# A planner for attention beside a gated FFN: later exponentials, limited chains, a load in seven parts

## The chip, the core and the metric

The kernel runs on one core of a Trainium2 chip. The core has five engines, each with its own instruction stream: TensorE (PE in the profile, with PEld for its weight loads) multiplies matrices into PSUM, VectorE (DVE) and ScalarE (ACT) read PSUM and SBUF, GpSimd (POOL) and SyncE (SP) here mostly issue DMAs. The engines run side by side and meet at semaphores. Within one stream the order is fixed when the program is built: an instruction that waits holds up all that stand behind it.

The metric is device time in microseconds. Thirteen runs of the kernel before gave a median of 865.38 us, from 860.25 to 869.33.

## What is computed

```python
qkv = (x @ wqkv).reshape(B, S, 3, H, Dh)          # S 2048, D 512, H 32, Dh 16
p = softmax(q @ k.T * Dh ** -0.5)                  # 32 heads of 2048 x 2048
a = (p @ v).reshape(B, S, D) @ wo
b = (silu(x @ w_gate) * (x @ w_up)) @ w_down       # F 1792
g = sigmoid((x * gate_w).sum(-1, keepdims=True))
out = g * a + (1 - g) * b
```

The heads are narrow (16), so the 32 x 2048 x 2048 exponentials outweigh the matmuls: 134 million elements of softmax on a core whose engines handle 128 of them side by side.

## The kernel before, in words

**Units, slots, blocks.** The queries are cut into 4 blocks of 512, the heads into 8 groups of 4. A unit is one query block with one head group; there are 32 (`UNIT`, L114). A unit has 16 slots, one for each 128 keys, so `SLOTS` is 512. A slot has four score blocks of 128 keys x 512 queries, one for each head. `score` (L656) is one matmul of 64 rows; two heads sit in the two row halves of the array, so two such matmuls run side by side.

**Two ways to an exponential.** `emit_pair` (L669) puts two score blocks into one PSUM tile `s_t` (two buffers) and lets ACT take the exponential of 128 x 1024 elements at once into `e_t` (ten buffers). `emit_d` (L688) puts a block into one of the three spare PSUM banks as `d_t`, and DVE makes the exponentials of a whole slot (128 x 2048) itself: four steps y_t<-d_t, one for each block, which scale the scores into the bits of a bf16; then the correction z_t, u_t<-z_t, two 128 x 2048 products, a DMA of POOL that adds u_t onto y_t, and a last step y_t<-y_t. The scratch u_t changes place from one tile to the next: a buffer of its own, or by turns another tensor that is not in use yet or any more: `wd_t[:, 0:4]` up to unit 4, then `kaug[:, 0]` (L712).

**What each unit ends with.** `pv` (L774) multiplies the exponentials of a slot with V (o_ps<-e_t or o_ps<-y_t, four heads side by side). After 16 slots `close` (L1047) copies o_ps into osb on DVE, and SP copies the rows of osb to where they are needed.

**Chains.** All other matmuls are cut into pieces of one or two matmul steps and put between the score pairs: projections of K, V and Q for later units (`k_pieces`, L393; its copy goes to `kst`, for most groups the tensor `on`, and eight DMAs on SP bring it into `kaug`, L420), the bounds of the exponents, the gate, the FFN's gate and up products (`gu_chain`, L596, 8 steps in two banks, then a tanh on ACT and two DVE steps gs and mt), the down products (`down_pieces`, L627, 28 steps in two banks) and the output projection (`fin_pieces`). `Pacer` gives every slot a credit, from the work that is left and its deadlines. A chain with a tanh needs ACT between exponentials.

**The planner.** One Python loop (L1186 on) writes out the whole order for PE, ACT and DVE before anything runs; `ordered` (L145) then ties each instruction to the one before it on its engine. The loop keeps an estimate of when each engine is done (`plan.pe`, `plan.act`, `plan.dve`) from fixed durations: an exponential 0.905 us (`emit_pair`), a tanh 0.48 (`done_gu`, L608), DVE's steps 0.6 to 1.2. From these it decides how much fits between two score pairs (`room`, then `side`, L1108), when a bank is free (`m_tile`, `m_free`), when `pv` may go (`e_end`), and how many slots of a unit DVE takes: `v_unit` (L1153) gives DVE a slot only while DVE's estimated end, with 16 us to spare, lies before ACT's. So a changed duration changes the share of the work and the order on every engine.

The DMAs of SP and POOL are not tied this way. They stand in an order that follows from the program and from what they wait for, and each waits in its own queue for its operands and for one of eight completion semaphores, which go round. `wd_load` (L202, called from `begin`, L1089, at slot 88) fetches the down weights; it is later than it need be for the FFN because `wd_t[:, 0:4]` serves as scratch until then.

The lines that the change touches: `wd_load` L202, `done_gu` L608, `emit_pair` L669, the costs in `emit_d` L716 to L731, `begin` L1083, `side` L1108, `next_pv` L1130, and the main loop.

Of the kernel before, what the change touches and what calls it, by code (L numbers as in the profile page):

```python
# [8 lines left out]
ACT = mybir.ActivationFunctionType  # L9
# [69 lines left out]
def kernel(  # L79
# [12 lines left out]
    nc = tc.nc  # L92
# [66 lines left out]
    def act(*args, **kw):  # L159
        ordered(nc.scalar.activation(*args, **kw))  # L160
# [38 lines left out]
                h = H - 8 + 4 * i + j  # L199
                nc.sync.dma_start(out=wo_l[32 * j + 1:32 * j + 1 + DH, i, :], in_=A_wo[h * DH:(h + 1) * DH, :])  # L200

    def wd_load():  # L202
        nc.sync.dma_start(out=wd_t[:], in_=B_w_down.rearrange("(fc p) d -> p fc d", p=P))


    kaug = big.tile([P, G, S], BF16, name="kaug")
# [389 lines left out]
    def gu_chain(qb, fc):  # L596
        st = {}

        def load():
            st["wg"] = ffnw.tile([P, DC, P], BF16, tag="wg", name="wg")  # L600
            nc.sync.dma_start(out=st["wg"][:], in_=B_w_gate[:, fc * P:(fc + 1) * P].rearrange("(dc p) f -> p dc f", p=P))
            st["wu"] = ffnw.tile([P, DC, P], BF16, tag="wu", name="wu")
            nc.sync.dma_start(out=st["wu"][:], in_=B_w_up[:, fc * P:(fc + 1) * P].rearrange("(dc p) f -> p dc f", p=P))

        def rows(which):
            return lambda dc: (st["w" + which][:, dc, :], xT[:, dc, qb * QBW:(qb + 1) * QBW])

        def done_gu(gp, up):  # L608
            th = work.tile([P, QBW], BF16, tag="th", name="th")
            act(out=th[:], in_=gp[:, :], func=ACT.Tanh, scale=0.5)  # L610
            plan.act = max(plan.act, plan.pe + 0.25) + 0.48

            def gate():
                st["gs"] = work.tile([P, QBW], BF16, tag="gs", name="gs")
                vec.scalar_tensor_tensor(out=st["gs"][:], in0=th[:], scalar=1.0, in1=gp[:, :],
                                         op0=ALU.add, op1=ALU.mult)
                m_free(gp, plan.dve)

            def gated():
                vec.scalar_tensor_tensor(out=mt[:, fc, :], in0=st["gs"][:], scalar=0.5, in1=up[:, :],  # L620
                                         op0=ALU.mult, op1=ALU.mult)
                m_free(up, plan.dve)
            later(0.6, gate, plan.act + 0.2)
            later(0.6, gated, plan.act + 0.2)
        return load, two_banks(DC, "gu", rows("g"), rows("u"), done_gu)
# [43 lines left out]
    def emit_pair(bs):  # L669
        i = pairs[0] % 2  # L670
        s_t = ps_s.tile([P, 2 * QBW], F32, tag="s", name="s_t")
        e_t = etp.tile([P, 2 * QBW], BF16, tag="e", name="e_t")
        for k, b in enumerate(bs):
            score(s_t[:, k * QBW:(k + 1) * QBW], b)
            e_of[b] = e_t[:, k * QBW:(k + 1) * QBW]
        spend("R", 1, s_end[i])
        act(out=e_t[:], in_=s_t[:], func=ACT.Exp, scale=inv_sqrt_dh)
        plan.act = max(plan.act, plan.pe + 0.27) + 0.905
        s_end[i] = plan.act + 0.18
        for b in bs:  # L680
            e_end[b] = plan.act + 0.25
            e_left[b] = pairs[0]
        pairs[0] += 1

    d_wait = []
    y_live = [0]

    def emit_d():  # L688
        if not vcur:
            vcur.update(n=v_take(), i=0, y=vex.tile([P, NV * QBW], U16, tag="y", name="y_t", bufs=NY))  # L690
            y_live[0] += 1
        n, i, y = vcur["n"], vcur["i"], vcur["y"]
        vcur["i"] += 1
        d_t = m_tile("d_t")
        score(d_t[:, :], 4 * n + i)
        spend("R", 1)
        e_of[4 * n + i] = y[:, i * QBW:(i + 1) * QBW].bitcast(BF16)
        if i == NV - 1:
            vcur.clear()

        def first():
            vec.tensor_scalar(out=y[:, i * QBW:(i + 1) * QBW], in0=d_t[:, :], scalar1=EXP_A, scalar2=EXP_B,
                              op0=ALU.mult, op1=ALU.add)
            m_free(d_t, plan.dve)
            if i < NV - 1:
                return
            z = vex.tile([P, NV * QBW], U16, tag="z", name="z_t")
            u_turn[0] ^= 1
            if u_turn[0]:

                ua = (kaug[:, 0, :] if au > QB else wd_t[:, 0:4, :].rearrange("p f d -> p (f d)")).bitcast(F16)
            else:  # L712
                ua = vex.tile([P, NV * QBW], F16, tag="u", name="u_t")[:, :]
            ya, za = y[:, :], z[:, :]
            vops.extend([
                (0.66, lambda: vec.tensor_scalar(out=za, in0=ya, scalar1=0x1FF, scalar2=0x800, op0=ALU.bitwise_and,  # L716
                                                 op1=ALU.bitwise_or)),
                (0.66, lambda: vec.tensor_scalar(out=ua, in0=za, scalar1=EXP_K, scalar2=EXP_M, op0=ALU.mult,
                                                 op1=ALU.add)),
                (1.2, lambda: vec.tensor_tensor(out=ua, in0=ua, in1=ua, op=ALU.mult)),  # L720
            ])

            def add():
                vec.tensor_tensor(out=ua, in0=ua, in1=za, op=ALU.mult)
                nc.gpsimd.dma_start(out=ya, in_=ua, accum_op=ALU.add)  # L725
                added.append((plan.dve + ADD_US, last))

            def last():
                vec.tensor_scalar(out=ya, in0=ya, scalar1=EXP_D, scalar2=0.25, op0=ALU.add, op1=ALU.mult)
                vready.append((plan.dve + 0.4, n))  # L730
            vops.append((1.2, add))  # L731
        d_wait.append((plan.pe + 0.25, first))

    def pay_d():
# [348 lines left out]
    def begin(n):  # L1083
        plan.slot = n
        for c in need.get(n, []):
            force(c)
        if n == 28:
            late_loads()
        if n == (QB + 1) * KT + 8:  # L1089
            wd_load()  # L1090
        for f in at.pop(n, []):
            f()
        pace.begin_slot(n)
# [14 lines left out]
    def side(most):  # L1108

        due = any(not c.out() for n in range(plan.slot, plan.slot + 12) for c in need.get(n, []))  # L1110
        cur = pace.cur
        begun = cur is not None and not cur.out() and cur.i
        c = pick() if pace.credit > 0 or due or begun else None
        if c is None:
            return None
        mms, _, takes = c.pieces[c.i][:3]
        mode, two = c.pieces[c.i][3:] or ("F", None)
        if two and two["seq"] == plan.seq:
            return None
        t = m_ready(int(takes)) if takes else 0.0  # L1120
        if t is None or t > plan.pe + 0.1 or 0.226 * mms + (0.1 if plan.mode != mode else 0.0) > most:
            return None
        return c
# [4 lines left out]
        pace.credit -= emit_piece(c)  # L1128

    def next_pv():  # L1130
        while not pv_list(None):
            if vops:
                pay_v()
            elif d_wait:
                pay_d()
            elif owed:
                pay()
            elif added:
                pay_a()
            else:  # L1140
                emit_d()
        emit_pv(pv_list(None)[0])
# [43 lines left out]
    while au < UNITS:  # L1186
        if plan.slot < au * KT + at_ * KT // hi[au]:
            begin(plan.slot + 1)
            continue
        fill_dve()  # L1190
        back = pairs[0] - min(e_left.values(), default=pairs[0])
        if back >= EB - 1:
            next_pv()
            continue
        room = s_end[pairs[0] % 2] - plan.pe
        if room > 0.02:
            if want_d():
                emit_d()
                continue
            n_pv = pv_list(plan.pe)  # L1200
            switch = 0.0 if plan.mode == "C" else 0.1
            fits = int((room + SLACK - switch) / 0.216)
            c = side(room + SLACK)
            if n_pv and fits > 0 and (plan.mode == "C" or len(n_pv) > 1 and fits > 1 and (pv_turn[0] or c is None)
                                      or back >= EB - 4 or c is None and fits == 1):
                emit_pv(n_pv[0])
                pv_turn[0] = False
                continue
            if c is not None:
                put_piece(c)  # L1210
                pv_turn[0] = True
                continue
            if room > 0.15:
                plan.pe += 0.1
                continue
        n = au * KT + at_
        emit_pair([4 * n + 2 * half, 4 * n + 2 * half + 1])
        half ^= 1
        at_ += not half
        forward()  # L1220
    while closed < UNITS or vops or added or vcur:
        fill_dve()
        while owed and owed[0][0] <= plan.pe:
# [90 lines left out]
```

## Time and profile before

| | us |
|---|---|
| median of 13 runs | 865.38 |
| the profiled execution, as timed | 862.26 |
| its span, first to last instruction | 860.5 |
| first exponential of the main loop starts | 22.98 |
| last one ends | 849.49 |
| ACT busy | 819.4 |
| DVE busy | 789.4 |
| PE busy | 769.7 |
| mean granted TensorE clock | 0.976 of full speed |

The profile is of one execution. Its page gives busy time by engine, then by groups of like instructions: line, engine, operation, output<-input, shapes, count, then busy time, the mean length of one, the idle time just before them and what ended it. All instructions of PE, ACT and DVE carry the line of the helper that records them (L157, L160, L166), so the groups are told apart by their tiles. The lengths of neighbours overlap on ACT and DVE: the busy time of a group divided by its count is nearer to what one costs than its mean length. A row of a wait reads: who waited for whom, the sum, the number of times, the longest. The granted clock is given as a share of full speed, by stretches.

### The profile page before, as it was taken

Reading aid. Unit: us, or ns where it says so; the run is one execution under the profiler, and the core shown is the slowest. Engines: PE = TensorE matmul, PEld = TensorE weight load, DVE = VectorE, ACT = ScalarE, POOL = GpSimd, SP = SyncE. Lnnn points to the kernel's source line nnn. Section 1 sums busy time; section 2 is a strip of 40 time slices with the busy share of each in tenths; the row PEclk is TensorE's granted clock in tenths of the full one; section 3 lists DMA queues with packets and bytes.
Section 4 is the critical chain, followed back from the end, with each engine's and each line's share of the span. In section 5 each row is a group of like instructions: output and inputs, shape, how many; then the busy total and the mean of one; then the engine's idle time right before and its main releaser. Section 6 shows DMA issues by size and latency. Waiting matters only on the chain.

```text
span 860.5 us, 16031 instructions
## 1 busy us (share of the span) xinstructions
PE 769.7 (89%) x5964; PEld 261.4 (30%) x5964; DVE 789.4 (92%) x1137; ACT 819.4 (95%) x917; POOL 93.0 (11%) x118
## 2 busy tenths in 40 slices
PE   5999998899899998898899889998998889999975
PEld 2222232223233323333333233322333223333311
DVE  7999997789989999998999899999999989999993
ACT  3999999799999999999999899999999999999994
POOL 3010010000101111100011111010101100101100
PEclk9999999899999999999999899999999999999978
DMA  8232437244545246535333534545334554433422
GB/s 202 62 70 45 77 66 175 59 100 86 109 86 95 55 88 131 102 87 102 79 70 61 119 91 97 113 92 104 72 69 84 111 102 100 94 77 61 92 44 55
DMA packets 100902, 77.16 MB, mean 90 GB/s; under 512 B 77504, under 2 KB 89368, under 8 KB 100824
## 3 DMA queue, kind: packets, MB, share of 16 engines
q0 software_dynamic: 12384, 45.09, 28.1%
q1 hardware_dynamic: 86712, 30.73, 14.6%
q8 instruction: 46, 0.75, 0.3%
q10 hardware_dynamic: 1728, 0.33, 0.2%
q14 instruction: 32, 0.26, 0.1%
HBM read 20.83 MB, written 2.34 MB: 27 GB/s over the span
## 4 chain that ended last, share of the span: by engine, by line
DVE 38%; PE 30%; ACT 21%; issue 6%; DMA 3%; SPq 1%; DVEq 0%; ACTq 0%
ACT e_t L160 19%; DVE y_t L166 12%; PE s_t L157 10%; DVE kaug L166 6%; DVE u_t L166 6%; PE o_ps L157 5%; DVE z_t L166 3%; PE d_t L157 3%; DVE mt L166 3%; DVE gs L166 2%; PE dps_b L157 2%; ACT th L160 2%; PE dps_a L157 2%; PE gu_b L157 2%; PE gu_a L157 1%
## 5 line engine op out<-in xcount | busy, mean ns | idle before, releaser
L160 ACT ACTIVATE e_t<-s_t 128x1024 bf16<-128x1024 f32 x852 | 797.4, 1114 | 17.8 <-PE s_t L157 17.2
L157 PE MATMUL s_t<-qx,kaug 64*128 64x512 bf16 x1380 | 294.6, 388 | 41.5 <-ACT e_t L160 36.7
L157 PEld LDWEIGHTS <-kaug 64*128 64x128 bf16 x2048 | 140.1, 93 | 338.6 <-issue 302.3
L166 DVE TENSOR_SCALAR y_t<-d_t 128x512 uint16<-128x512 f32 x344 | 225.4, 683 | 16.4 <-PE d_t L157 14.2
L157 PE MATMUL o_ps<-e_t,vaug 128*32 128x512 bf16 x1704 | 160.7, 394 | 1.3 <-ACT e_t L160 0.7
L157 PE MATMUL gu_a<-xT,wg 64*128 64x512 bf16 x448 | 140.9, 385 | 0.0
L157 PE MATMUL gu_b<-xT,wu 64*128 64x512 bf16 x448 | 138.0, 383 | 2.0 <-DVE y_t L166 1.3
L157 PE MATMUL d_t<-qx,kaug 64*128 64x512 bf16 x284 | 106.5, 380 | 13.1 <-DVE on L166 5.5
L157 PEld LDWEIGHTS <-vaug 128*32 128x32 bf16 x2048 | 43.8, 94 | 136.8 <-issue 134.8
L725 POOL DMA_DIRECT2D y_t<-kaug x37 | 38.3, 1034 | 363.6 <-PE s_t L157 172.2
L725 POOL DMA_DIRECT2D y_t<-u_t x43 | 39.4, 915 | 311.7 <-DVE u_t L166 119.1
L157 PE MATMUL dps_b<-wd_t,mt 64*128 64x512 bf16 x224 | 65.6, 375 | 0.5 <-DVE y_t L166 0.2
L157 PE MATMUL dps_a<-wd_t,mt 64*128 64x512 bf16 x224 | 65.9, 376 | 0.0
L166 DVE TENSOR_SCALAR z_t<-y_t 128x2048 uint16<-128x2048 uint16 x86 | 59.5, 692 | 2.1
L166 DVE TENSOR_SCALAR y_t<-y_t 128x2048 uint16<-128x2048 uint16 x86 | 58.6, 683 | 0.5 <-DMA y_t<-kaug 0.5
L166 DVE TENSOR_TENSOR u_t<-u_t 128x2048 f16<-128x2048 f16 x43 | 52.6, 1223 | 1.2
L157 PE MATMUL s_t<-q,kaug 64*128 64x512 bf16 x216 | 45.4, 386 | 8.6 <-ACT e_t L160 8.0
L166 DVE TENSOR_TENSOR u_t<-u_t,z_t 128x2048 f16<-128x2048 f16 x43 | 52.3, 1216 | 0.1
L157 PEld LDWEIGHTS <-wg 64*128 64x128 bf16 x448 | 41.9, 96 | 24.4 <-issue 13.1
L157 PEld LDWEIGHTS <-wu 64*128 64x128 bf16 x448 | 42.1, 95 | 17.6 <-issue 2.7
L166 DVE TENSOR_TENSOR kaug<-kaug 128x2048 f16<-128x2048 f16 x37 | 45.3, 1224 | 1.1
L166 DVE TENSOR_TENSOR kaug<-kaug,z_t 128x2048 f16<-128x2048 f16 x37 | 45.0, 1217 | 0.1
(116 smaller groups left out, 619.3 us busy)
## 6 DMA issues: line engine op xcount, KB each, us to landing
y_t<-u_t POOLq DMA_DIRECT2D x43, 512.0 KB, 4.8
y_t<-kaug POOLq DMA_DIRECT2D x37, 512.0 KB, 5.0
wg<-in_B_w_gate_dram SPq DMA_DIRECT2D x56, 128.0 KB
wu<-in_B_w_up_dram SPq DMA_DIRECT2D x56, 128.0 KB
y_t<-wd_t POOLq DMA_DIRECT2D x6, 512.0 KB, 4.7
on<-osb SPq DMA_DIRECT2D x120, 16.0 KB
rb<-rr SPq DMA_DIRECT2D x15, 128.0 KB
wd_t<-in_B_w_down_dram SPq DMA_DIRECT2D x1, 1792.0 KB
```

Source lines behind the costliest of these rows:

```text
L157: return ordered(nc.tensor.matmul(*args, **kw))
L160: ordered(nc.scalar.activation(*args, **kw))
L166: return lambda *a, **kw: ordered(f(*a, **kw))
L725: nc.gpsimd.dma_start(out=ya, in_=ua, accum_op=ALU.add)
```

## The change

Four things change; the computation stays the same.

1. `emit_pair` no longer puts the exponential into ACT's order at once. It puts it on a list `exps`; `flush_act` moves it to the order later: before the next pair, before a `pv`, as soon as the planner's clock says that it could begin, and at the ends. `done_gu` first moves those that could begin before the tanh is ready, then places the tanh, so that a tanh goes ahead of an exponential that has to wait.
2. `side` lets a begun chain go on without credit only down to a credit of -3.
3. `wd_load` loads two of the 14 chunks, and is called seven times, at every fourth slot from 88 on.
4. The planner's durations: an exponential 0.935 for 0.905, the free time of its score buffer 0.15 for 0.18 after it, of its result 0.22 for 0.25; DVE's steps 0.64 for 0.66 and 1.17 for 1.2.

```diff
-    def wd_load():
-        nc.sync.dma_start(out=wd_t[:], in_=B_w_down.rearrange("(fc p) d -> p fc d", p=P))
+    def wd_load(f):
+        nc.sync.dma_start(out=wd_t[:, f:f + 2, :], in_=B_w_down[f * P:(f + 2) * P, :].rearrange("(fc p) d -> p fc d", p=P))
...
             th = work.tile([P, QBW], BF16, tag="th", name="th")
+            flush_act(plan.pe + 0.2)
             act(out=th[:], in_=gp[:, :], func=ACT.Tanh, scale=0.5)
...
         spend("R", 1, s_end[i])
-        act(out=e_t[:], in_=s_t[:], func=ACT.Exp, scale=inv_sqrt_dh)
-        plan.act = max(plan.act, plan.pe + 0.27) + 0.905
-        s_end[i] = plan.act + 0.18
+        flush_act()
+        ready = plan.pe + 0.27
+
+        def exp():
+            act(out=e_t[:], in_=s_t[:], func=ACT.Exp, scale=inv_sqrt_dh)
+            plan.act = max(plan.act, ready) + ACT_US
+            s_end[i] = plan.act + 0.15
+            for b in bs:
+                e_end[b] = plan.act + 0.22
+        exps.append((ready, exp))
         for b in bs:
-            e_end[b] = plan.act + 0.25
             e_left[b] = pairs[0]
         pairs[0] += 1
+
+    exps = []
+    ACT_US = 0.935
+
+    def flush_act(before=None):
+
+        while exps and (before is None or max(plan.act, exps[0][0]) <= before):
+            exps.pop(0)[1]()
...
-                (0.66, lambda: vec.tensor_scalar(out=za, in0=ya, scalar1=0x1FF, scalar2=0x800, op0=ALU.bitwise_and,
+                (0.64, lambda: vec.tensor_scalar(out=za, in0=ya, scalar1=0x1FF, scalar2=0x800, op0=ALU.bitwise_and,
...
-                (1.2, lambda: vec.tensor_tensor(out=ua, in0=ua, in1=ua, op=ALU.mult)),
+                (1.17, lambda: vec.tensor_tensor(out=ua, in0=ua, in1=ua, op=ALU.mult)),
...
-        if n == (QB + 1) * KT + 8:
-            wd_load()
+        i = n - (QB + 1) * KT - 8
+        if 0 <= i < 2 * FC and i % 4 == 0:
+            wd_load(i // 2)
...
-        begun = cur is not None and not cur.out() and cur.i
+        begun = cur is not None and not cur.out() and cur.i and pace.credit > -3
...
     def next_pv():
+        flush_act()
         while not pv_list(None):
...
         fill_dve()
+        flush_act(plan.pe)
         back = pairs[0] - min(e_left.values(), default=pairs[0])
...
+    flush_act()
     while closed < UNITS or vops or added or vcur:
```

More of the change, by code (lines that the diff above doesn't have):

```diff
@@ L715, in first @@
             vops.extend([
-                (0.66, lambda: vec.tensor_scalar(out=za, in0=ya, scalar1=0x1FF, scalar2=0x800, op0=ALU.bitwise_and,
+                (0.64, lambda: vec.tensor_scalar(out=za, in0=ya, scalar1=0x1FF, scalar2=0x800, op0=ALU.bitwise_and,
                                                  op1=ALU.bitwise_or)),
-                (0.66, lambda: vec.tensor_scalar(out=ua, in0=za, scalar1=EXP_K, scalar2=EXP_M, op0=ALU.mult,
+                (0.64, lambda: vec.tensor_scalar(out=ua, in0=za, scalar1=EXP_K, scalar2=EXP_M, op0=ALU.mult,
                                                  op1=ALU.add)),
-                (1.2, lambda: vec.tensor_tensor(out=ua, in0=ua, in1=ua, op=ALU.mult)),
+                (1.17, lambda: vec.tensor_tensor(out=ua, in0=ua, in1=ua, op=ALU.mult)),
             ])
@@ L730, in last @@
                 vready.append((plan.dve + 0.4, n))
-            vops.append((1.2, add))
+            vops.append((1.17, add))
         d_wait.append((plan.pe + 0.25, first))
```

## The prediction

> **What bounds the kernel now.** I read the page first: which engine is busiest, and which groups carry it.
>
> ```profile
> PE 769.7 (89%) x5964; PEld 261.4 (30%) x5964; DVE 789.4 (92%) x1137; ACT 819.4 (95%) x917; POOL 93.0 (11%) x118
> L160 ACT ACTIVATE e_t<-s_t 128x1024 bf16<-128x1024 f32 x852 | 797.4, 1114 | 17.8 <-PE s_t L157 17.2
> L166 DVE TENSOR_SCALAR y_t<-d_t 128x512 uint16<-128x512 f32 x344 | 225.4, 683 | 16.4 <-PE d_t L157 14.2
> ```
>
> ACT is the busiest and it does almost nothing but exponentials. Neighbours overlap, so the cost of one is not its 1114 ns but the busy sum over the count: 797.4/852 = 0.936 us with the tails, and about 0.92 from start to start in the timeline (132 of them in 121.62 us). DVE is close behind: it makes 86 of the tiles of exponentials itself. So there are two bounds that share one pool of work, and the next view is what each of the two waits for.
>
> ```profile
> ACT e_t L160 <- PE s_t L157: 17.2, 19, 5.8
> ...
> DVE y_t L166 <- PE d_t L157: 14.2, 24, 1.4
> DVE on L166 <- DMA wu<-in_B_w_up_dram: 6.1, 1, 6.1
> DVE gs L166 <- ACT th L160: 4.7, 8, 1.0
> ```
>
> ACT loses 17.2 us in 19 waits for scores, and a third of that is one wait. The chain of waits, asked for 130 to 170 us alone, shows where that one comes from:
>
> ```profile
> 133.96 4.61 DMA y_t<-wd_t
> 138.63 9.43 DMA wd_t<-in_B_w_down_dram
> 148.08 4.32 DMA kaug<-on
> 152.66 0.70 DVE on L166
> 153.41 0.58 PE d_t L157
> ```
>
> The down weights cannot be loaded before the last scratch use of wd_t has landed. SP issues in order, so that load stands ahead of the eight K copies; the eighth copy waits until the load has landed, the copy of the next K tile into `on` waits for that copy, and behind it stand d_t, the scores and ACT. ("wu" in DVE's wait row is the inferred releaser; this chain names the copy.) On ACT's timeline:
>
> ```profile
> 154.51 2.12 ACT L160 ACTIVATE e_t<-s_t 128x1024 bf16<-128x1024 f32 x2 [5.76 <-PE s_t L157]
> 157.22 5.61 ACT L160 ACTIVATE e_t<-s_t 128x1024 bf16<-128x1024 f32 x6 [0.59 <-PE s_t L157]
> ```
>
> Most of the other waits lie where the granted TensorE clock had fallen (columns: stretch, its length, busy PE, PEld, DVE, ACT, POOL, then clock, DMA share, GB/s):
>
> ```profile
> 475.00:480.00 5.00, 2.86 (x22) 0.87 (x20) 3.96 (x6) 4.85 (x6) 0.86 (x1) 1.00 0.68 131
> 480.00:485.00 5.00, 4.96 (x26) 1.06 (x27) 4.97 (x8) 3.15 (x4) 0.00 (x0) 0.62 0.25 56
> 485.00:490.00 5.00, 4.86 (x37) 1.42 (x34) 3.52 (x5) 3.82 (x5) 1.17 (x1) 0.70 0.54 105
> ```
>
> PE is half idle for 5 us, then it gets 0.62 of its clock and ACT loses 3.2 us. Such places near 310, 485, 744 and 771 us cost ACT 0.84 + 3.18 + 0.86 + 0.60 = 5.5 us. The last view is the budget of the stretch from DVE's first tile of exponentials to the copy that closes the last unit but one:
>
> ```profile
> 24.50:826.60 802.10, 733.94 (x5701) 249.26 (x5699) 752.39 (x1063) 789.17 (x885) 81.44 (x84) 0.98 0.43 88
> ```
>
> There DVE is busy 752.4 of 802.1 us and ACT 789.2.
>
> **The change, part by part.** The sum is made against the profiled execution: span 860.5 us, 862.26 us as timed, 3.1 below the median of 865.38.
>
> *Seven parts for the down weights.* In the changed kernel's order on SP, five parts (all that miss the scratch, chunks 4 to 13) stand right after the first gate and up loads, issued near 24 us, when the DMA share falls to 0.10 (25 to 30 us); 1280 of the 1792 KB leave the critical place. The other two stand behind the eight q copies (qx<-qst) that follow the K copies, so they wait for scratch that has landed by then. Seven issues of about 0.4 us take the place of one on a queue that is mostly empty. Gone: 5.76 + 0.59 = 6.35 us of ACT. What is late next: the eight K copies still need 5.55 us to issue (the undisturbed eight at 185 us) and at most the 4.32 us to land shown above, 9.9 together; on DVE some 8.2 us of other work lie between the two K tiles in the new order (two y_t, z, u, a square, the 2.28 us reduction, gs, mt, y). So 0 to 1.7 us come back; I take 0.7, since 4.32 was measured beside the big load. Net -5.6.
>
> *Six exponentials fewer on ACT.* Counted in both orders: e_t 852 to 846, y_t 344 to 356, so 86 DVE tiles become 89. This follows from the planner's new durations (0.935 for 0.905 on ACT; DVE's steps cheaper). ACT: 6 x 0.92 = -5.5 us. PE and the 56 tanhs are unchanged in count. DVE per tile, busy sum over count: 4 x 0.655 + 0.69 (z) + 0.73 (u) + 1.22 + 1.22 + 0.68 = 7.16; three are +21.5 us. POOL issues three more adds of about 1 us on an engine that is 11% busy.
>
> *Tanh ahead of the waiting exponential.* The number of ACT instructions stays. gs and mt come up to 0.9 us earlier, so two PSUM banks come free earlier; at best DVE's 4.7 us on th vanish. At worst ACT stands idle for a late last gate matmul while scores wait: the nearest row is a step of a gate/up pair, 0.21 us, on 56 places, 12 us. The planner lets the tanh ahead only where the exponential could not yet have begun, so I take 0 on ACT and -3 on DVE's waits.
>
> *Chain bursts limited.* I laid the PE steps from the chain (0.21 for a pair of row halves, 0.33 for four o_ps after a change of layout) on the two orders. Stretches of four score pairs with less than 0.55 us of PE work per pair: before, 7 in the body and 11 at the end; after, none in the body and 4 at the end. The dips that go before the low clock should mostly go: of 5.5 us I take -3.5 (bounds -5.5 and 0). The price is that a down chain holds two of three banks for 20.75 score pairs in the mean instead of 15.25, 8 x 5.5 x 0.92 = 40 us more in all; DVE in such a stage (265 to 300 us) is busy 92% against 94% over the body, so about 1 us. Gate/up chains get shorter (3.8 for 4.1 pairs).
>
> A rule speaks against this step. The Trainium skill, "TensorE: Matmul & The Clock Gate", section "What's actually happening", says that the clock falls after at least one idle window of about 3.4 us. In the rows above it fell to 0.62 when no PE gap was over 0.71 us, so here a half idle window was enough. By the rule, filling short gaps would bring 0 instead of -3.5, and ACT's side below would come to -11.1 instead of -14.6.
>
> *ACT's side alone:* -5.6 - 5.5 - 3.5 = -14.6 us.
>
> *DVE's side.* With none of its waits left, DVE's body takes 752.4 busy + 8.9 (its gaps under 0.1 us between dependent steps) + 21.5 + about 2 (work moved ahead of the close) = 784.8, so it ends at 24.5 + 784.8 = 809.3. Five more score pairs follow the close than before (25 for 20 behind `dl`), so ACT's end lies 22.9 + 5 x 0.92 = 27.5 us later, at 836.8 against 849.5: -12.7. Of DVE's 37.6 us of waits in the body, the K copy's 6.1 and 3 of the tanh's go; 28.5 could stay. A DVE that is late waits less for d_t, but the order is fixed and PE stalls with it. Its best 50 us stage (650 to 700) was 98% busy, the mean one 94%. At 98% the stretch of 784.8 less the small gaps, 775.9, takes 791.7 (+6.9 of waits); at 96% it takes 808.2 (+23.4). I take the best stage, since DVE will have work in hand nearly always, rounded down to 6: -12.7 + 6 = about -7. The tail of 11 us behind the last exponential is the same work.
>
> DVE decides, so the sum is -7: 862.3 - 7 = 855.3 for an execution like the profiled one, 858 for the median.
>
> **The rivals.** (1) *ACT stays the bound*: DVE finds room without waits, as at 300 to 350 and 650 to 700 us. Both sides then give -13 to -14.6: 851. For it: ACT pitch and DVE floor allow it. Against: DVE at over 99% for 800 us, which no 50 us stage shows. (2) *No change to speak of*: 13 us of DVE's waits survive and eat the whole gain; 865. (3) *Slower, DVE becomes the bound with its old waits*: the 24 waits for d_t and those on q and bound tiles all stay, w = 20 to 28, and the end moves by -12.7 + w = +7 to +15: 873 to 880. It decides from w = 12.7 us. For it: the planner counts a DVE tile as 4 x 0.6 + 2 x 0.64 + 2 x 1.17 + 0.63 = 6.65 us where the rows give 7.16, 89 x 0.5 = 45 us of busy time that it does not see, though overlap hides part. Against: most waits for d_t arise where PE waits for ACT, and ACT has less to do. (4) *The split changes nothing*, because the copies' own issue and landing hold the K tile anyway: 6 us of the sum come back. DVE's wait goes with it, so this is case 2.
>
> **How the numbers follow.** About 0.3% (2.6 us) is what a measurement of this kernel can tell from no change. Forecast, -7 with its own range 851 to 863: 0.48. Rival 1, 851: 0.18. Rivals 2 and 4, within 2.6 us: 0.12. Rival 3: 0.22. Faster 0.66, same 0.12, slower 0.22. The range runs from 847 (rival 1 with the last low-clock waits gone too) to 873, the near end of rival 3.
>
> **What would show it.** ACT's long wait near 150 us and DVE's 6.1 us wait gone, with K copies issued without a gap; e_t x846 near 792 us; DVE busy near 811 us and 94 to 95% of the span; the waits of y_t for d_t under 10 us; clock of 1.00 through the body; gs waiting for th under 2 us. I am wrong if DVE's waits add up to over 13 us in the body, if PE's waits for DVE (6.2 us for d_t now) multiply, or if ACT's wait for scores is over 17 us again.

## The result, and the profile after

The changed kernel takes 874.66 us in the median of 11 runs (870.09 to 877.82). Beside it 48 runs of the kernel before gave 865.01 us. The ratio is 1.0107, 95% interval 1.0083 to 1.0132: slower by about 9 us, where 7 us faster had been forecast. The profiled execution has a span of 874.3 us against 860.5, 13.8 us more.

From the page of the changed kernel, the busy times and the groups of ACT's exponentials and of DVE's first step:

```profile
PE 772.7 (88%) x5964; PEld 253.6 (29%) x5964; DVE 805.8 (92%) x1164; ACT 822.8 (94%) x911; POOL 93.4 (11%) x121
L160 ACT ACTIVATE e_t<-s_t 128x1024 bf16<-128x1024 f32 x846 | 796.9, 1066 | 25.9 <-PE s_t L157 22.3
L166 DVE TENSOR_SCALAR y_t<-d_t 128x512 uint16<-128x512 f32 x356 | 233.4, 683 | 17.1 <-PE d_t L157 15.1
```

The counts are those that the prediction had counted in the order, 846 and 356. But six exponentials fewer took only 0.5 us off the group's busy time, not 5.5: its instructions overlap less, because more of them start late. ACT's waits for scores did not fall, although the great wait near 150 us is gone. They are 42 short ones:

```profile
ACT e_t L160 <- PE s_t L157: 22.3, 42, 1.4
PE d_t L157 <- DVE y_t L166: 17.8, 46, 1.1
DVE y_t L166 <- PE d_t L157: 15.1, 26, 1.0
PE d_t L157 <- DVE gs L166: 5.5, 12, 0.7
DVE gs L166 <- ACT th L160: 3.6, 3, 2.0
```

The second row is the new thing. PE waits for DVE to free the bank of a d_t 46 times for 17.8 us; before it was 16 times for 6.2 us. All of PE's waits of over 0.15 us for DVE add up to 54 us in 121 places, against 29 us in 46 (about 6 us of each sum is one wait at the start of the kernel, and 5.5 of the 29 belonged to the load). DVE waits for d_t as long as before, 15.1 us against 14.2.

One such place, in the order of time. PE's rows (start, length, what, and in brackets the idle time before and what ended it):

```profile
760.51 0.37 PE L157 MATMUL d_t<-qx,kaug 64*128 64x512 bf16 x1 [0.56 <-DVE y_t L166]
762.24 0.37 PE L157 MATMUL d_t<-qx,kaug 64*128 64x512 bf16 x1 [0.70 <-DVE gs L166]
763.03 1.01 PE L157 MATMUL qp<-xT,wqk 128*128 128x512 bf16 x2 [0.20 <-DVE mt L166]
```

and ACT's in the same stretch:

```profile
764.68 1.02 ACT L160 ACTIVATE e_t<-s_t 128x1024 bf16<-128x1024 f32 x1 [0.73 <-PE s_t L157]
766.63 2.11 ACT L160 ACTIVATE e_t<-s_t 128x1024 bf16<-128x1024 f32 x2 [0.92 <-PE s_t L157]
769.65 2.90 ACT L160 ACTIVATE e_t<-s_t 128x1024 bf16<-128x1024 f32 x3 [0.91 <-PE s_t L157]
```

DVE is late, PE stands at the next bank with the scores queued behind, and ACT starves. The windows (stretch, length, busy PE, PEld, DVE, ACT, POOL, clock, DMA share, GB/s) show the second half of the price:

```profile
760.00:765.00 5.00, 3.58 (x19) 0.70 (x18) 4.67 (x7) 4.09 (x6) 0.86 (x1) 0.79 0.38 73
765.00:770.00 5.00, 5.00 (x27) 0.81 (x26) 2.90 (x6) 3.10 (x4) 0.00 (x0) 0.53 0.58 98
```

Three short stops in 3 us, and the granted clock falls to 0.53; now DVE and ACT both wait for slow matmuls. The same happened near 150, 245 and 515 us: stops of PE for DVE of 0.2 to 1.6 us, then a stretch of 5 us at 0.69, 0.50 and 0.50. Together the four places hold 10.5 of ACT's 22.3 us.

The budget of the body, from 24.5 us to the copy that closes the last unit but one, and of what comes behind it:

```profile
24.50:837.30 812.80, 735.26 (x5683) 239.93 (x5682) 772.74 (x1094) 788.79 (x874) 82.95 (x88) 0.98 0.44 90
837.30:861.90 24.60, 18.80 (x153) 6.24 (x152) 12.88 (x20) 24.54 (x27) 0.86 (x1) 1.00 0.11 22
861.90:874.30 12.40, 4.17 (x30) 1.63 (x29) 3.90 (x9) 0.69 (x1) 1.27 (x1) 0.64 0.12 42
```

DVE's body takes 812.8 us instead of 802.1: 20.3 us more work, 9.6 us less idle time. DVE's waits of over 0.15 us in the body add up to 27.9 us where they were 37.6. The K copy's 6.1 us are gone; the waits for d_t, the largest group, are not. ACT was busy 98.4% of the body before and is busy 97.0% of it now.

### The profile page after: what moved, and what is told of

Same layout as the page of the kernel before. It is cut to its first block, busy times and chain, and to the rows that moved or that the text cites. A ratio compares the mean times of both kernels' runs of the same rounds, so it can differ in the third digit from the quotient of the medians.

```text
span 874.3 us, 16036 instructions
## 1 busy us (share of the span) xinstructions
PE 772.7 (88%) x5964; PEld 253.6 (29%) x5964; DVE 805.8 (92%) x1164; ACT 822.8 (94%) x911; POOL 93.4 (11%) x121
## 5 line engine op out<-in xcount | busy, mean ns | idle before, releaser
L160 ACT ACTIVATE e_t<-s_t 128x1024 bf16<-128x1024 f32 x846 | 796.9, 1066 | 25.9 <-PE s_t L157 22.3
L157 PE MATMUL s_t<-qx,kaug 64*128 64x512 bf16 x1368 | 302.7, 386 | 30.2 <-ACT e_t L160 27.4
L166 DVE TENSOR_SCALAR y_t<-d_t 128x512 uint16<-128x512 f32 x356 | 233.4, 683 | 17.1 <-PE d_t L157 15.1
L157 PEld LDWEIGHTS <-kaug 64*128 64x128 bf16 x2048 | 131.1, 93 | 314.3 <-issue 272.1
L157 PE MATMUL d_t<-qx,kaug 64*128 64x512 bf16 x296 | 109.8, 384 | 23.5 <-DVE y_t L166 14.7
L740 POOL DMA_DIRECT2D y_t<-kaug x38 | 36.1, 951 | 337.9 <-PE s_t L157 184.9
L157 PE MATMUL dps_b<-wd_t,mt 64*128 64x512 bf16 x224 | 67.5, 375 | 1.1 <-DVE y_t L166 0.7
L157 PE MATMUL dps_a<-wd_t,mt 64*128 64x512 bf16 x224 | 68.2, 376 | 0.0
L166 DVE TENSOR_SCALAR z_t<-y_t 128x2048 uint16<-128x2048 uint16 x89 | 61.6, 692 | 1.9
L166 DVE TENSOR_SCALAR y_t<-y_t 128x2048 uint16<-128x2048 uint16 x89 | 61.0, 685 | 1.0 <-DMA y_t<-u_t 0.9
L157 PE MATMUL s_t<-q,kaug 64*128 64x512 bf16 x216 | 50.1, 388 | 3.9 <-ACT e_t L160 3.6
L157 PEld LDWEIGHTS <-wg 64*128 64x128 bf16 x448 | 41.1, 95 | 27.5 <-issue 15.5
L157 PEld LDWEIGHTS <-wu 64*128 64x128 bf16 x448 | 41.7, 95 | 24.5 <-issue 7.2
```

The costliest lines, as they stand in the source:

```text
L157: return ordered(nc.tensor.matmul(*args, **kw))
L166: return lambda *a, **kw: ordered(f(*a, **kw))
```

## The experiments

All ratios are to runs of the kernel before on the same chip, with 95% intervals. "Rest" below means the late exponentials, the chain limit and the load in seven parts together. The planned costs of one DVE tile over one exponential, 6.75/0.905 = 7.46 before and 6.65/0.935 = 7.11 in the changed kernel, are called the plan's ratio.

**The load in seven parts alone.**

```diff
-        if n == (QB + 1) * KT + 8:
-            wd_load()
+        i = n - (QB + 1) * KT - 8
+        if 0 <= i < 2 * FC and i % 4 == 0:
+            wd_load(i // 2)
```

> The kernel before with the down weights loaded in seven parts and nothing else. Tiles of exponentials on DVE stay at 86. All theories that hold the stall at 148 to 154 us for removed: ratio 0.993, about 859 us against 865, ACT's 5.76 us wait and DVE's 6.1 us wait gone. If the copies of K hold the tile by themselves, or the time gained is given back by other waits: 1.000.

Measured: 0.9918 (0.9884 to 0.9951), 856.94 us. ACT's timeline has no gap left where 5.76 and 0.59 us stood:

```profile
145.55 11.21 ACT L160 ACTIVATE e_t<-s_t 128x1024 bf16<-128x1024 f32 x12
156.45 0.81 ACT L160 ACTIVATE th<-gu_a 128x512 bf16<-128x512 f32 x1
156.93 11.33 ACT L160 ACTIVATE e_t<-s_t 128x1024 bf16<-128x1024 f32 x12
```

SP's rows say why: the two parts that still stand ahead of the copies carry 512 of the 1792 KB, and the eight copies go out in 4.99 us where they took 9.04.

```profile
139.37 0.95 SPq L203 DMA_DIRECT2D wd_t<-in_B_w_down_dram  x2
140.42 4.99 SPq L420 DMA_DIRECT2D kaug<-on  x8
```

This part is worth 7 us (4 to 10 by the interval), where 5.6 was forecast.

**The late exponentials alone.** The kernel before with `exps`, `flush_act` and its five calls, at the old durations.

> The kernel before with the late exponentials alone: durations, chain limit and the one load of the down weights as before, 86 tiles. Theory 'share': 1.000 within 0.004, the stall near 150 us still there. Theory 'late': 1.007 or more.

Measured: 0.9976 (0.9948 to 1.0005), 862.04 us. The stall near 150 us is still there (5.42 us). The tanh goes ahead without harm to ACT, and gs waits 3.1 us instead of 4.7.

**The changed kernel without the chain limit.**

```diff
-        begun = cur is not None and not cur.out() and cur.i and pace.credit > -3
+        begun = cur is not None and not cur.out() and cur.i
```

> The changed kernel without the limit on begun chains; the planner then gives DVE 90 tiles. Theory 'share': ratio 1.010 to 1.016. Theory 'limit': 0.993 to 1.000, and PE's wait for DVE at d_t falls from 17.8 us to under 9.

Measured: 1.0119 (1.0065 to 1.0172). DVE makes 90 tiles here. The limit is not what costs, and it brings nothing that can be told either: with it the ratio is 1.0107.

**The changed kernel with the planner's old durations.**

```diff
-    ACT_US = 0.935
+    ACT_US = 0.905
-            s_end[i] = plan.act + 0.15
+            s_end[i] = plan.act + 0.18
-                e_end[b] = plan.act + 0.22
+                e_end[b] = plan.act + 0.25
...
-                (0.64, lambda: vec.tensor_scalar(out=za, in0=ya, scalar1=0x1FF, scalar2=0x800, op0=ALU.bitwise_and,
+                (0.66, lambda: vec.tensor_scalar(out=za, in0=ya, scalar1=0x1FF, scalar2=0x800, op0=ALU.bitwise_and,
```

> The changed kernel with all the planner's durations of before, so DVE takes 86 tiles and not 89; late exponentials, chain limit and seven parts stay. Theory 'share' (three more tiles on a DVE that had no room): ratio 0.990 to 0.997, PE's wait for DVE at d_t back under 9 us. Rivals 'limit' (down chains hold two banks for longer) and 'late' (a tanh ahead of an exponential makes ACT wait): 1.007 or more, as the changed kernel.

Measured: 0.9887 (0.9834 to 0.9940), 854.51 us. So the rest wins 1.1% and the durations lose 2.2%.

**The durations alone, on the kernel before.**

> The kernel before with the new durations alone: 91 DVE tiles, 842 exponentials; one load of the down weights, no limit, exponentials as before. Theory 'share' at 7 us for a tile: five tiles more, +35 us less the 9 us of exponentials that may come free, ratio 1.03 to 1.04; at least 1.015. Rival 'limit' or 'late' as causes of the loss: 1.00.

Measured: 1.0284 (1.0257 to 1.0312), 888.99 us. PE's waits for DVE add up to 62 us. The loss is the durations'. My first theory of how, the number of tiles ('share'), made the next run.

**The changed kernel with 86 tiles.** `LEAD` is 28 instead of 16: DVE gets a slot only if it ends 28 us ahead of ACT.

> The changed kernel with all its durations, and LEAD 28 in place of 16, which gives DVE 86 tiles again. Theory 'share' (the number of DVE tiles decides): ratio 0.988 to 0.995. Rival 'order' (the longer ACT duration lets the planner put more PE work between score pairs than fits, whatever the number of tiles): 1.003 or more, ACT's waits for scores over 15 us.

Measured: 1.0228 (1.0193 to 1.0263), 884.96 us. With the tiles of the kernel before, but the new durations, it is slower still, so the number of tiles alone does not set the time.

```profile
ACT e_t L160 <- PE s_t L157: 25.0, 50, 3.1
PE d_t L157 <- DVE y_t L166: 11.4, 30, 0.8
```

DVE is busy only 790.3 us here, as before, and PE waits for it 45 us in 98 places. But the run changes LEAD as well, and LEAD is no neutral knob, as the next run shows. Why it is slower than with LEAD 16 stays open, so it does not clear 'share' of a part in the loss.

**Old durations with 88 and with 84 tiles.** LEAD 4 instead of 16 in the one, an exponential planned at 0.890 in the other.

> Old durations, with late exponentials, limit and seven parts, and LEAD 4 in place of 16: 88 DVE tiles. Theory 'share' at 7 us for a tile: two more tiles than the run with old durations at 0.989, so 1.003 to 1.008. Rival 'order': 0.985 to 0.995.

> Old durations, with late exponentials, limit and seven parts, and an exponential planned at 0.890: 84 DVE tiles, 856 exponentials on ACT. If DVE is the bound at 86 tiles as well: 14 us less on DVE, ratio 0.972 to 0.980. If ACT bounds there: four exponentials more, 0.989 to 0.996.

Measured: 1.1169 (1.1139 to 1.1199) and 0.9985 (0.9966 to 1.0005). The first misses both theories by far and says nothing on tiles; what it took away was DVE's spare time:

```profile
PE o_ps L157 <- DVE y_t L166: 65.7, 22, 6.1
```

At the ends of the units PE stands before DVE's last tiles, in 22 places. The second misses its two ranges too. It lost 8.3 us of ACT in one such wait (o_ps for y_t, 7.0 us at about 56 to 63 us) that the plan with 0.905 does not have. Fewer tiles were no gain here.

**What in the durations?** The theory that was left, 'pace': each step of the plan couples the three engines. If it holds an exponential for longer than it is, it puts more DVE work between two of them than fits; DVE's steps then end later than planned, and PE, whose order is fixed, stands before banks that the plan had counted as free. So the ratio of DVE's times to ACT's should decide. The same ratio also sets the number of tiles that DVE gets, so a run that moves it moves both. In the trace of before, 556 of the 795 distances between the starts of neighbouring exponentials are 0.900 to 0.909 us, the median 0.904; the same distances on DVE, where no wait lies between, are 4 x 0.616 + 0.71 + 0.75 + 1.15 + 1.17 + 0.61 = 6.85 us for a tile. The real ratio is 7.58. The change moved the plan away from it.

One duration at a time, on the rest with old durations: the exponential, DVE's steps, the two ends.

> Old durations but for one: an exponential planned at 0.935 instead of 0.905; late exponentials, limit and seven parts stay. 89 tiles. Theory 'pace' (the plan gives DVE more time between two exponentials than ACT's real pitch of 0.904 leaves, so DVE's steps come late and PE stands behind them): ratio 1.00 to 1.01, PE's waits for DVE (25 us with old durations, 54 in the changed kernel) over 40. If the other durations carry it: 0.985 to 0.995.

> The changed kernel with ACT's old durations (0.905, 0.18, 0.25); only DVE's steps are planned at 0.64 and 1.17. 86 tiles. Theory 'pace': a fourth of the change in the ratio of the two, so 0.988 to 0.998. If DVE's steps carry the loss: 1.005 or more.

> Old durations, with late exponentials, limit and seven parts; only the two ends behind an exponential are new (0.15 and 0.22). 86 tiles. Theory 'pace': no effect, 0.985 to 0.995. If it is the earlier end of the score buffer that puts PE in the wrong order: 1.005 or more.

Measured: 1.0002 (0.9980 to 1.0024), 0.9921 (0.9891 to 0.9951) and 0.9868 (0.9816 to 0.9921). Against 0.9887, the exponential loses 1.2%; DVE's steps lose 0.3% and the ends nothing, both within the noise. That is about 1.5 of the 2.2%; the rest shows only with all of them together, and no run says why. Then the cross tests. The changed kernel with its exponential at 0.935, but with all DVE durations times 1.05:

```diff
-        plan.dve = max(plan.dve, ready) + cost
+        plan.dve = max(plan.dve, ready) + cost * 1.05
...
-        plan.dve = max(plan.dve, ready) + 0.6
+        plan.dve = max(plan.dve, ready) + 0.6 * 1.05
...
-        plan.dve += cost
+        plan.dve += cost * 1.05
...
-        plan.dve = max(plan.dve, ready) + 0.63
+        plan.dve = max(plan.dve, ready) + 0.63 * 1.05
```

> The changed kernel with every DVE duration of the planner times 1.05, which brings the ratio of a DVE tile to an exponential back to that of before (6.98 to 0.935 as 6.75 to 0.905). 85 tiles. Theory 'pace': 0.985 to 0.998, PE's waits for DVE under 35 us. Rival 'order' by the exponential's 0.935 itself (PE's own filling of a pair that is too long): 1.005 or more.

Measured: 0.9882 (0.9838 to 0.9926), 854.96 us, with 85 tiles. The exponential's 0.935 does no harm once DVE's times go with it:

```profile
PE d_t L157 <- DVE y_t L166: 5.4, 13, 1.4
ACT e_t L160 <- PE s_t L157: 4.3, 7, 1.5
```

And the mirror, the exponential at 0.905 and DVE's times at 0.955:

> Old durations (exponential 0.905), every DVE duration of the planner times 0.955: the ratio of the changed kernel without its 0.935. 90 tiles. Late exponentials, limit and seven parts stay. Theory 'pace': 1.005 to 1.02, PE's waits for DVE over 40 us. Rival 'the exponential's 0.935 itself': 0.985 to 0.998.

Measured: 1.0078 (1.0055 to 1.0101), with 90 tiles. With the old exponential most of the loss is back. The last three look for the best ratio.

> The changed kernel with every DVE duration times 1.04: 87 tiles. Theory 'pace': between the changed kernel and 1.05, nearer to the latter: 0.986 to 0.996.

> The changed kernel with every DVE duration times 1.07: 85 tiles. Theory 'pace': PE's waits for DVE are no longer what costs, 0.982 to 0.992; slower than with 1.05 if DVE's idle time now lies on ACT's path.

> The run with the two new ends alone (0.987), with every DVE duration times 1.02. 85 tiles. Theory 'pace': PE's waits for DVE fall below 25 us and the time stays at 0.98 to 0.99, since ACT gets two exponentials more (1.8 us).

Measured: 0.9916 (0.9892 to 0.9940), 0.9941 (0.9912 to 0.9969, slower than expected) and 0.9842 (0.9805 to 0.9878). All runs with late exponentials, limit and seven parts and LEAD 16, by the plan's ratio:

| plan's ratio | run | DVE tiles | PE's waits for DVE, us | time to before |
|---|---|---|---|---|
| 7.11 | the changed kernel | 89 | 54 | 1.0107 |
| 7.12 | old exponential, DVE x 0.955 | 90 | 53 | 1.0078 |
| 7.22 | exponential 0.935 alone | 89 | 44 | 1.0002 |
| 7.35 | DVE's steps alone | 86 | 36 | 0.9921 |
| 7.40 | changed, DVE x 1.04 | 87 | 25 | 0.9916 |
| 7.46 | old durations | 86 | 25 | 0.9887 |
| 7.46 | the two ends alone | 86 | 27 | 0.9868 |
| 7.47 | changed, DVE x 1.05 | 85 | 18 | 0.9882 |
| 7.58 | exponential 0.890 | 84 | 30 | 0.9985 |
| 7.61 | changed, DVE x 1.07 | 85 | 21 | 0.9941 |
| 7.61 | the two ends, DVE x 1.02 | 85 | 15 | 0.9842 |

About 6 us of each sum of waits is the one at the start of the kernel; only in the rows of DVE x 1.04 and x 1.05 does the profile put that one down to a DMA.

Up to 7.47 the time falls with the ratio, whichever of the two durations makes it; the last three rows up to there, 7.46 and 7.47, cannot be told apart. Beyond, near the real 7.58, it depends on the single plan. So the ratio is what costs. The table does not say by which of its two effects, because the number of tiles falls as the ratio rises, from 89 or 90 in the first three rows to 84 to 87 in the others. DVE's body, from 24.5 us to its closing copy, says more:

| run | DVE tiles | DVE busy, us | its waits of over 0.15 us | smaller gaps | body, us | ACT busy in it |
|---|---|---|---|---|---|---|
| the changed kernel | 89 | 772.7 | 27.9 | 12.2 | 812.8 | 97.0% |
| exponential 0.935 alone | 89 | 773.3 | 19.0 | 12.9 | 805.2 | 98.0% |
| old durations | 86 | 754.9 | 23.1 | 13.0 | 791.0 | 99.1% |
| changed, DVE x 1.05 | 85 | 748.0 | 30.4 | 13.1 | 791.5 | 99.4% |
| changed, LEAD 28 | 86 | 760.1 | 52.3 | 12.8 | 825.2 | 96.7% |

Between the changed kernel and the old durations lie 21.8 us. DVE's work makes 17.8 of them and its waits 4.8; the waits of the fast x 1.05 are no shorter. By this account most of the loss is 'share': DVE got three tiles more and had no room for them. That tiles are not all is seen at equal numbers: with 89 the time is 1.0107 or 1.0002, with 86 it is 1.0228 (LEAD 28) or 0.9868 to 0.9921. 'Pace' fits these, but no run holds tiles and LEAD fixed and moves the ratio from 7.46 to 7.11, so how much is pace stays open.

The fastest is the last row, 850.47 us: 1.6% faster than the kernel before and 2.6% faster than the changed one by the two ratios (0.9842/1.0107 = 0.974). It is the best of several plans tried, and its interval overlaps those of the two ends alone and of DVE x 1.05. It keeps the change's first three parts, the two new ends and the old exponential, and plans DVE's steps a little longer, not shorter.

## Why the prediction was wrong

The forecast was -7 us; measured were +13.8 in the span and about +9.6 between the medians (the profiled executions lie 2.8 us below and 2.9 us above theirs), inside the price of rival 3 (+7 to +15) and above the stated range. All three signs of being wrong came: DVE's waits in the body were 27.9 us (over 13), PE's waits for y_t to free a d_t bank went from 6.2 to 17.8 us, and ACT's waits for scores were 22.3 us (over 17).

- *The bound and the great wait.* Right. The load's place held the K copies, and its split is worth 7 us by its own run; -5.6 was forecast.
- *Six exponentials fewer, -5.5.* Wrong in kind: a shorter list of work is a gain on ACT only while scores come in time. The group's busy time fell by 0.5 us and its waits for scores grew from 17.2 to 22.3 us, though 6.35 of the old ones had gone.
- *Tanh ahead, 0 on ACT and -3 on DVE's waits.* The step alone gives 0.9976 with an interval that just holds 1, so 0 on ACT is not contradicted. It takes 1.6 us off gs, and in the changed kernel the wait is 1.1 us shorter: about half of the 3 or less.
- *Chain limit, -3.5 by the clock.* Wrong. The mean granted clock is 0.977 against 0.976, and without the limit nothing changes. Behind the close of the body the clock did rise, from 0.72 to 1.00, but it is 1.00 there without the limit too. At the old durations the seven parts and the late exponentials together come to 0.9918 x 0.9976 = 0.9894 by their own runs, and with the limit to 0.9887: no gain that can be told. My count of thin stretches in the order saw only where PE has little to do, not where it will be held; the new stops lowered the clock again. The rows keep their quarrel with the Trainium skill, "TensorE: Matmul & The Clock Gate", section "What's actually happening", which asks for an idle window of about 3.4 us: at 760 to 770 us no gap shown for PE is over 0.70 us, and the clock fell to 0.53.
- *DVE's side: -12.7 + 6.* This is the step that failed. The floor of the body was put at 809.3 us without waits and 6 us of waits were added, from the best 50 us stage. The floor was right: busy time and smaller gaps came to 772.7 + 12.2 = 784.9 us, for 784.8. The body closed at 837.3, so the waits were 28, and the trace has 27.9: very nearly the 28.5 that "could stay". The term of 6 was mis-sized, and it measured 28. DVE was busy 95.1% of its body, not the 98% of its best stage. Behind it ACT needed 24.6 us for 27.5, and the tail 12.4 for 11.0: -12.7 + 28 - 2.9 + 1.4 = +13.8. The prediction named the reason, "PE stalls with it", but gave it no price and took 6 because DVE would have work in hand. The runs show PE's waits for DVE grown from 29 to 54 us, and DVE's waits for d_t as long as before (15.1 us for 14.2). That the first keep up the second is the likely link; it is argued from places like the one at 760 us, not shown as a sum.
- *Rival 3* had the right price and, as far as the runs go, the right account: DVE becomes the bound with its old waits, w = 27.9 us. The planner's tile that is too cheap is a part of the cause, but only in its ratio to the exponential: with 0.935 the kernel is fast when DVE's times rise along with it. Rival 3 did not see that PE's waits for DVE would double.
- What I did not do: hold the planner's new 0.935 against the trace of before. I took 0.92 from start to start for a price, a mean in which late starts count; most distances were near 0.904, so the old 0.905 was the measured duration and the new one was not. That 0.935 is the busy time over the count (797.4/852 = 0.936) may be where it comes from; nothing here shows it.

## What to carry to other kernels

An order that is fixed ahead from planned durations is sensitive to their ratio: here 4.7% in the ratio of two durations was worth 2% of the time. An engine that is planned too slow hands work to its neighbour, and the plan may also pack that work too densely. The delay then returns as many waits of half a microsecond at shared buffers, not as one long one. Take such durations from the distance of starts where nothing waits, not from busy time over count or from means with waits in them, and compare them with the trace before the planner's new split of the work is priced. When a changed planner gives an engine more to do, price its old idle time as staying, and look for what its lateness holds up.

## What the runs showed of the chip that I had not expected

The granted clock of TensorE falls without a long pause: with three stops of 0.56, 0.70 and 0.20 us within 3 us it was 0.79 in the stretch of 5 us that holds them and 0.53 in the next. The sum of PE's waits does not set the mean clock, though: the last row of the table and DVE x 1.05, with 15 and 18 us of them, had 0.992 and 0.994, but DVE's steps alone had 0.994 with 36 us, and the split 0.977 with 21 us.

The exponential of 128 x 1024 starts every 0.904 us when its scores are there, while one lasts 1.02 to 1.31 us: neighbours overlap by a tenth of a microsecond and more, and the mean length in the groups went from 1114 to 1066 ns as the kernel got slower. Those that start alone last about 1.02 us (764.68 us above), so a shorter mean here is a sign of late starts, not of faster work.
